# Sliding-window attention and a SwiGLU block: the second half of the output weights issued directly behind the first

## The chip, the cores and the metric

The kernel runs on one core of a Trainium2 chip. The core has five engines that work side by side, each through its own queue, strictly in order: TensorE (PE in the profile; PEld is its weight load), VectorE (DVE), ScalarE (ACT), GpSimd (POOL) and SyncE (SP). Sixteen DMA engines move data between the device's memory and the on-chip memory. The metric is the device time of one execution in microseconds.

## The reference

Two stages follow one another. The first is attention with a sliding window of 128 positions and a linear bias, over 8 batches, 8 heads, 576 positions and a head width of 64:

```
scores = q @ k^T / sqrt(64) - slope[head] * |i - j|, only where 0 <= i - j < 128
x = softmax(scores) @ v, brought to [4608 tokens, 512]
```

The second is a gated feed-forward block on those 4608 tokens, with an inner width of 1536:

```
g = x @ w_gate
out = (g * sigmoid(g) * (x @ w_val)) @ w_out
```

Inputs and output are 32-bit floats; the kernel computes in 16-bit floats and accumulates in 32 bits.

## The kernel before, in words

**Attention.** The sequence is cut into tiles of 128 positions. Two batches together make 9 tiles (four of each batch, and a ninth that holds the last 64 positions of both), so the 8 batches give 36 tiles, numbered 0 to 35 ("rank" in the code). For every tile the kernel loads k, q and v (`load_qk`, L187 to L192, and `load_v`, L182 to L185). k and q have to be transposed. Tiles 0 to 10 are transposed by TensorE (`transposed`, L198 to L223, with the products at L218); from tile 11 on, a DMA transpose does it, issued by SyncE (L239). Then come the scores (L278 and L313), the exponential on ScalarE (L284, L317), the weighting with v (L345), the division on VectorE (L348), and the transpose of the result into xT (L371 or L367).

**Feed-forward.** Tokens go in 9 blocks of 512. Each block has 12 strips of the inner width; a strip is one gate product and one value product (L397), an activation (L415) and two VectorE operations (L416, L427). Block 0's output product is done plainly (`project`, L446 to L457): 12 products per output tile with the 12 strips of w_out, taken from the last strip to the first:

```
m = NMB - 1 - i if n == 0 else i
nc.tensor.matmul(po, hT[n][:, m, j * P:(j + 1) * P], wo_sb[:, m, :],
```

So block 0 reads strips 11 to 6 of `wo_sb` first (its second half by position, `wo_sb[:, 6:12]`), and then strips 5 to 0. Later blocks use a scheme with seven products in place of eight (`strassen`, L504, products at L532); it needs sums of the output weights, which VectorE makes from both halves (`weight_sums`, L468 to L478).

**The order of the work.** The loads of the first eleven tiles and of all weights are issued by GpSimd, in an order that is written out by hand (L876 to L909). Each load names its destination, and the built program lets it wait for what that destination still needs: k and q go into five buffers each in turn, v into twelve. Each load also reports its completion on one of eight semaphores in turn; a load waits until the eighth load before it has landed. On the other engines the order of the first part is the order of the code, and later a scheduler has placed the instructions; TensorE's interleaving of attention and feed-forward comes from the counts in `everything` (L936 to L971). From tile 11 on, `loads_to` (L779) adds a tile's loads as attention proceeds.

The two halves of the output weights are 768 KB each on the chip (128 partitions, 6 strips, 512 columns, 16 bits). The first to be loaded is `wo_sb[:, 6:12]` (L902). Then k and q of tile 9 and q of tile 10 are loaded, then `wo_sb[:, 0:6]` (L905), then v of tile 9, and k and v of tile 10.

Of the kernel before, what the change touches and what calls it, by code (L numbers as in the profile page):

```python
# [51 lines left out]
def kernel(  # L52
# [10 lines left out]
    nc = tc.nc  # L63
# [69 lines left out]
    wo_sb = consts.tile([P, NMB, DM], FP16, name="wo_sb")  # L133
    wg2 = moe_w_gate.rearrange("(kb p) f -> p kb f", p=P)
    wv2 = moe_w_val.rearrange("(kb p) f -> p kb f", p=P)
    wo2 = moe_w_out.rearrange("(a p) d -> p a d", p=P)
# [36 lines left out]
    def source(src, rank):  # L173

        s, c = divmod(rank, 9)
        if c == 8:
            return [((64 * n, 64 * n + 64),
                     src[2 * s + n, :, 512:576, :].rearrange("h p d -> p h d")) for n in range(2)]
        b, t = 2 * s + c // 4, c % 4
        return [((0, P), src[b, :, t * P:(t + 1) * P, :].rearrange("h p d -> p h d"))]  # L180

    def load_v(rank):  # L182
        va[rank] = va_all[rank % NV]
        for (p0, p1), src in source(v, rank):
            nc.gpsimd.dma_start(va[rank][p0:p1, :, 0:D], src)  # L185

    def load_qk(rank, which="kq"):  # L187
        for name in which:
            t_ = nat.tile([P, H, D], FP16, name=name + "n", tag=name + "n")
            for (p0, p1), src in source(k if name == "k" else q, rank):  # L190
                nc.gpsimd.dma_start(t_[p0:p1], src)  # L191
            (natk if name == "k" else natq)[rank] = t_  # L192

    def load(rank):
        load_qk(rank)
        load_v(rank)
# [703 lines left out]
    load_v(7)  # L900
    load(8)
    nc.gpsimd.dma_start(wo_sb[:, 6:12, :], wo2[:, 6:12, :])  # L902
    load_qk(9)
    load_qk(10, "q")
    nc.gpsimd.dma_start(wo_sb[:, 0:6, :], wo2[:, 0:6, :])  # L905
    load_v(9)
    load_qk(10, "k")
    load_v(10)
# [96 lines left out]
```

## Time and profile before

| | us |
|---|---|
| median of 4 runs | 346.74 (346.18 to 348.81) |
| profiled execution, its own time | 345.66 |
| its span, first to last instruction | 343.9 |
| TensorE busy | 330.2 (96%) |
| VectorE busy | 277.3 (81%) |
| ScalarE busy | 207.6 (60%) |
| GpSimd busy (issuing loads) | 109.6 (32%) |
| output weights, issue to landing, median of the two halves | 8.7 |
| k or q of a tile (128 KB), issue to landing, median | 8.5 |

The granted TensorE clock is 1.0 throughout. The DMA engines are busy for 9 tenths or more in each of the first 20 of the span's 40 equal slices, that is for about 172 us, and little afterwards. Busy times overlap between engines and do not add up to the span. In the chain that ended last, a piece of an engine or of a transfer says what released the next instruction, not how long that instruction stood still; how long it stood is in the list of waits. In a row of the timeline the columns are start, length, engine, line, operation, output <- inputs, count, and in brackets the engine's idle time just before the row and what ended it.

### The profile page before, as it was taken

To read this page: it belongs to the slowest core of one execution; us is meant where nothing else is said; L and a number is where in the kernel's file an instruction comes from. 1 tells how busy PE (TensorE), PEld (TensorE's weight loads), DVE (VectorE), ACT (ScalarE), POOL (GpSimd) and SP (SyncE) were. 2 spreads that over 40 slices of the span, in tenths; PEclk is the share of its full clock that TensorE was granted. 3 is DMA by queue.
4 is the path that set the end of the run, shared out by engine and by line. 5 is a ranking of instruction groups with operands and counts; after the bars stand their busy time and mean duration, and the time that the engine had idled before them with its cause. 6 is when DMAs were issued, how large, how long until landed. Compare 5 with 4: busy or idle time off the path is not lost.

```text
span 343.9 us, 7777 instructions
## 1 busy us (share of the span) xinstructions
PE 330.2 (96%) x2983; PEld 219.0 (64%) x2983; DVE 277.3 (81%) x652; ACT 207.6 (60%) x412; POOL 109.6 (32%) x136
## 2 busy tenths in 40 slices
PE   7999989999999999999999999999999999999995
PEld 4484445444456565556565655565788878888884
DVE  5577885999798679998899999999855975775683
ACT  3758676465766665656556547563467666676640
POOL 8977590748855075743017000000000000000000
PEclk9999999999999999999999999999999999999999
DMA  9999999999999999999949914021101101011024
GB/s 151 168 180 175 161 173 149 99 137 180 126 171 150 162 149 171 152 154 149 196 112 92 183 36 79 15 64 45 63 2 61 62 0 64 8 56 63 0 71 115
DMA packets 160037, 37.37 MB, mean 109 GB/s; under 512 B 147328, under 2 KB 155648, under 8 KB 160000
## 3 DMA queue, kind: packets, MB, share of 16 engines
q0 software_dynamic: 118336, 18.62, 85.2%
q1 hardware_dynamic: 40976, 17.64, 27.7%
q10 hardware_dynamic: 688, 0.62, 0.6%
q8 instruction: 23, 0.38, 0.5%
q14 instruction: 14, 0.11, 0.2%
HBM read 37.91 MB, written 9.44 MB: 138 GB/s over the span
## 4 chain that ended last, share of the span: by engine, by line
PE 70%; DVE 18%; ACT 5%; issue 3%; DMA 3%; POOL 0%; DVEq 0%; ACTq 0%
PE po L532 14%; PE pg L397 12%; PE pv L397 12%; PE gX L623 8%; PE gY L623 4%; PE av L345 3%; DVE hT L427 3%; DVE uu L416 3%; DMA wo_sb<-in_moe_w_out_dram 3%; PE ps L278 3%; PE p L532 3%; PE gZ L623 2%; PE po L451 2%; ACT ex L284 2%; DVE x L348 2%
## 5 line engine op out<-in xcount | busy, mean ns | idle before, releaser
L397 PE MATMUL pv<-xT,wv_sb 128*128 128x512 f16 (+2 forms) x320 | 76.5, 358 | 0.6 <-DVE uu L416 0.3
L397 PE MATMUL pg<-xT,wg_sb 128*128 128x512 f16 (+2 forms) x320 | 75.8, 358 | 0.3 <-DVE xT L373 0.2
L415 ACT ACTIVATE tt<-pg 128x512 f16<-128x512 f32 (+2 forms) x70 | 41.3, 590 | 50.5 <-PE pg L397 49.5
L284 ACT ACTIVATE ex<-ps 128x512 f16<-128x512 f32 x96 | 50.0, 606 | 11.8 <-PE ps L278 11.8
L416 DVE SCALAR_TENSOR_TENSOR uu<-tt,pg 128x512 f16<-128x512 f16 (+2 forms) x69 | 46.0, 667 | 10.4 <-ACT tt L415 10.2
L427 DVE TENSOR_TENSOR hT<-uu,pv 128x512 f16<-128x512 f16 (+2 forms) x70 | 46.7, 667 | 3.3 <-PE pv L397 1.6
L185 POOL DMA_DIRECT2D va<-in_v_dram x40 | 34.4, 865 | 38.8 <-PE av L345 30.5
L397 PEld LDWEIGHTS <-wg_sb 128*128 128x128 f16 x320 | 28.2, 98 | 24.4 <-issue 2.2
L397 PEld LDWEIGHTS <-wv_sb 128*128 128x128 f16 x320 | 28.3, 98 | 24.1 <-issue 3.0
L532 PEld LDWEIGHTS <-hT 128*128 128x128 f16 x384 | 36.8, 98 | 10.4 <-issue 1.1
L191 POOL DMA_DIRECT2D kn<-in_k_dram x39 | 33.5, 862 | 22.2 <-DMA kT<-kn 13.8
L191 POOL DMA_DIRECT2D qn<-in_q_dram x39 | 33.6, 866 | 15.1 <-DMA va<-in_v_dram 11.1
L532 PEld LDWEIGHTS <-S 128*128 128x128 f16 x288 | 27.7, 98 | 10.6 <-issue 2.5
L290 DVE TENSOR_TENSOR ex<-ex,m_reg 128x1024 f16<-128x1024 f16 x42 | 28.7, 688 | 3.2 <-ACT ex L284 3.1
L348 DVE TENSOR_TENSOR x<-av,rec 128x256 f16<-128x256 f32 x72 | 28.5, 419 | 0.4
L532 PE MATMUL po<-T,S 128*128 128x256 f16 x192 | 26.5, 273 | 0.5 <-DVE S L487 0.5
L532 PE MATMUL po<-T,hT 128*128 128x256 f16 x192 | 26.1, 273 | 0.0
L317 ACT ACTIVATE exc<-psc 128x512 f16<-128x512 f32 x40 | 21.3, 608 | 4.1 <-PE psc L313 4.1
L675 DVE TENSOR_TENSOR hT<-s,v 128x512 f16<-128x512 f16 x18 | 7.6, 424 | 18.5 <-ACT s L674 18.5
L345 PEld LDWEIGHTS <-ex 128*128 128x128 f16 x384 | 17.4, 97 | 4.6 <-issue 1.3
L345 PE MATMUL av<-va,ex 128*128 128x65 f16 x384 | 19.3, 194 | 0.7 <-ACT ex L284 0.7
L278 PE MATMUL ps<-qT,kT 64*128 64x256 f16 x192 | 16.6, 273 | 0.4 <-DVE qT L223 0.2
(134 smaller groups left out, 537.7 us busy)
## 6 DMA issues: line engine op xcount, KB each, us to landing
out_dram<-osb SPq DMA_DIRECT2D x32, 256.0 KB, 2.7
va<-in_v_dram POOLq DMA_DIRECT2D x32, 128.0 KB, 8.9
qn<-in_q_dram POOLq DMA_DIRECT2D x31, 128.0 KB, 8.5
kn<-in_k_dram POOLq DMA_DIRECT2D x31, 128.0 KB, 8.5
wg_sb<-in_moe_w_gate_dram POOLq DMA_DIRECT2D x6, 256.0 KB, 7.7
wv_sb<-in_moe_w_val_dram POOLq DMA_DIRECT2D x6, 256.0 KB, 8.2
wo_sb<-in_moe_w_out_dram POOLq DMA_DIRECT2D x2, 768.0 KB, 8.7
kn<-in_k_dram POOLq DMA_DIRECT2D x8, 64.0 KB, 7.4
```

What stands on the lines that cost most here:

```text
L185: nc.gpsimd.dma_start(va[rank][p0:p1, :, 0:D], src)
L191: nc.gpsimd.dma_start(t_[p0:p1], src)
L284: nc.scalar.activation(e[:, o:o + 2, :], banks[q4][par], AF.Exp, scale=scale)
L290: nc.vector.tensor_mul(e[:, o, :], e[:, o, :], reg[:, o, :])
L345: nc.tensor.matmul(av[:, j, :], w, val, start=(n == 0), stop=(n == len(todo) - 1))
L348: nc.vector.tensor_mul(x[:, 4 * half:4 * half + 4, :], av[:, :, 0:D], rec.broadcast_to([P, 4, D]))
L397: nc.tensor.matmul(ps[:, c0:c1], w[:, kb, ms], xT[n][:, kb, c0:c1], start=(kb == 0 and c0 == 0), stop=(kb == NKB - 1 and c1 == 512), skip_ ...
L415: nc.scalar.activation(tt, pg[:, c0:c1], AF.Tanh, scale=0.5)
L416: nc.vector.scalar_tensor_tensor(out=uu, in0=tt, scalar=one if (n, m) == PIN else 1.0, in1=pg[:, c0:c1], op0=ALU.add, op1=ALU.mult)
L427: nc.vector.tensor_mul(hT[n][:, m, c0:c1], acted[(n, m)][1][:, c0:c1], pv[:, c0:c1])
L532: nc.tensor.matmul(dst, a[:, m, cols], b[:, m, :], start=(start and m == 0), stop=(m == HM - 1), skip_group_check=True)
L623: nc.tensor.matmul(dst[:, i, :], w[:, kb, c0 + i * P:c0 + (i + 1) * P], a[:, kb, :], start=(start and i == 0 and kb == 0), stop=(i == 1 an ...
```

## The change

One line of the hand-written order moves up by two lines: the load of `wo_sb[:, 0:6]` is issued directly behind that of `wo_sb[:, 6:12]`, ahead of k and q of tile 9 and q of tile 10. Nothing else of the code changes. On GpSimd four loads change places; the order of instructions on the other engines stays as it was, and where one of them waits for one of these four loads, it waits on the semaphore of the load's new place.

```
     load_v(7)
     load(8)
     nc.gpsimd.dma_start(wo_sb[:, 6:12, :], wo2[:, 6:12, :])
+    nc.gpsimd.dma_start(wo_sb[:, 0:6, :], wo2[:, 0:6, :])
     load_qk(9)
     load_qk(10, "q")
-    nc.gpsimd.dma_start(wo_sb[:, 0:6, :], wo2[:, 0:6, :])
     load_v(9)
     load_qk(10, "k")
     load_v(10)
```

More of the change, by code (lines that the diff above doesn't have):

```diff
@@ L902 @@
     nc.gpsimd.dma_start(wo_sb[:, 6:12, :], wo2[:, 6:12, :])
+    nc.gpsimd.dma_start(wo_sb[:, 0:6, :], wo2[:, 0:6, :])
     load_qk(9)
     load_qk(10, "q")
-    nc.gpsimd.dma_start(wo_sb[:, 0:6, :], wo2[:, 0:6, :])
     load_v(9)
```

## The prediction

> **What bounds the kernel now.** I read the page first: how full each engine is, and what the chain that ended last consists of.
>
> ```profile
> PE 330.2 (96%) x2983; PEld 219.0 (64%) x2983; DVE 277.3 (81%) x652; ACT 207.6 (60%) x412; POOL 109.6 (32%) x136
> PE 70%; DVE 18%; ACT 5%; issue 3%; DMA 3%; POOL 0%; DVEq 0%; ACTq 0%
> ```
>
> TensorE is busy 96% of the 343.9 us, and 70% of the chain is its own work. A transfer is worth time only where TensorE stands waiting for it. The chain does contain one long transfer, and it is the one that this change moves; so the second view is the chain in order of time, around it.
>
> ```profile
> 43.48 1.40 POOL qn L191 x2
> 44.88 0.33 issue
> 45.21 9.51 DMA wo_sb<-in_moe_w_out_dram
> 54.72 0.04 issue
> 54.76 0.59 PE po L451 x2
> ```
>
> The piece of 9.51 us looks like the prize (2.8% of the span). It isn't one: the chain is followed back from whatever released an instruction last, however short the wait. The waits of TensorE between 40 and 60 us give the real size:
>
> ```profile
> PE px L371 <- DVE x L348: 0.8, 2, 0.6
> PE psc L313 <- ACT xT L375: 0.2, 1, 0.2
> PE po L451 <- DMA wo_sb<-in_moe_w_out_dram: 0.2, 1, 0.2
> ```
>
> One wait of 0.2 us. For nearly all of the 9.51 us TensorE had other work. Fourth view: the GpSimd queue, which issues every load and which the change reorders.
>
> ```profile
> 40.56 0.84 POOL L902 DMA_DIRECT2D wo_sb<-in_moe_w_out_dram  x1 [0.72 <-DMA wv_sb<-in_moe_w_val_dram]
> 42.60 0.88 POOL L191 DMA_DIRECT2D kn<-in_k_dram  x1 [1.21 <-PE ps L278]
> 43.48 1.76 POOL L191 DMA_DIRECT2D qn<-in_q_dram  x2
> 45.21 0.85 POOL L905 DMA_DIRECT2D wo_sb<-in_moe_w_out_dram  x1
> 46.02 0.92 POOL L185 DMA_DIRECT2D va<-in_v_dram  x1
> ...
> 48.90 0.88 POOL L191 DMA_DIRECT2D kn<-in_k_dram  x1 [0.21 <-PE av L345]
> 49.76 0.88 POOL L191 DMA_DIRECT2D qn<-in_q_dram  x1
> ```
>
> The first kn and the two qn are k of tile 9 and q of tiles 9 and 10; the last two rows are k and q of tile 11. Fifth view: when TensorE takes the things that trade places.
>
> ```profile
> 54.01 0.59 PE L451 MATMUL po<-wo_sb,hT 128*128 128x512 f16 x2
> 54.76 0.59 PE L451 MATMUL po<-wo_sb,hT 128*128 128x512 f16 x2 [0.15 <-DMA wo_sb<-in_moe_w_out_dram]
> 55.30 0.39 PE L218 MATMUL pt<-idm,kn 128*128 128x128 f16 x4
> 55.52 0.39 PE L218 MATMUL pt<-idm,qn 128*128 128x128 f16 x4
> 56.29 0.39 PE L218 MATMUL pt<-idm,qn 128*128 128x128 f16 x4
> ```
>
> The row at 54.76 is the first to use the half that is moved. Half a microsecond later come the transposes of k 9 and q 9, then q 10. So the change helps one use and endangers three right behind it on the same in-order engine.
>
> **The landings.** Issue plus time to landing, one load at a time: first half of the weights 40.56 + 7.8 = 48.4; k 9 42.60 + 6.6 = 49.2; q 9 43.48 + 6.6 = 50.1; q 10 44.34 + 6.5 = 50.9; second half 45.21 + 9.5 = 54.7; v 9 46.02 + 9.8 = 55.8; k 10 57.5; v 10 58.5; k 11 48.90 + 10.3 = 59.2; q 11 59.7; v 11 60.7. They land in the order of issue and the DMA engines read 9 tenths throughout: one backlog, worked off in order. What one load occupies is the distance between landings: the second half 54.7 - 50.9 = 3.8 us, and k 9, q 9, q 10 0.8, 0.9 and 0.8, together 2.5.
>
> **Part 1: the second half of the weights earlier (gain 0.25 us).** In the new order it waits for the completion of the eighth load before it (the built program puts each load on one of eight semaphores in turn). That is v 7, 33.01 + 9.1 = 42.1. It is issued at about 42.1 and joins a backlog that has 6 us left, so it follows the first half directly: 48.4 + 3.8 = 52.2 instead of 54.7. TensorE wants it at 54.4 (the pair at 54.01 at a pitch of 0.59 - 0.38 = 0.21 us each), so the wait goes. Its size is 0.15 us counted from the modelled end of the matmul before, 0.32 from the pitch. Next in line are the transposes of x at L371, whose input the trace has ready at 54.7, which caps the gain at 0.28. I take 0.25; below nothing is excluded for this term, since the wait only ends earlier.
>
> **Part 2: k 9, q 9, q 10 later (cost 0).** Behind the weights they land at 52.2 + 0.8 = 53.1, 53.9 and 54.7. TensorE, 0.25 us earlier than now, wants them at 55.0, 55.25 and 56.0. Margins: 1.9, 1.3 and 1.3 us. The cover is what TensorE does up to then; if it is gone, each microsecond of lateness is one of span, as TensorE is in order.
>
> [...]
>
> **Part 3: GpSimd's queue (cost 0).** One issue of 0.85 us moves ahead of three. GpSimd idles 1.21 us at that point anyway, waiting for TensorE to free k 9's buffer; the weights' issue fills 42.1 to 43.0, and k 9, q 9, q 10 are issued 0.4 us later, v 9 0.4 us earlier. All stand in the backlog for over 6 us, so this moves no landing.
> The turn of semaphores adds one wait: the load of q 11 waits for its eighth predecessor, which was k 9 (landed 49.2) and becomes the second half of the weights (52.2). So q 11 is issued at 52.3, not 49.76, and v 11 at about 53.2; behind them is k 12, which waits for the transpose of k 11 until 62.38 anyway. Their data's turn comes only after k 11, at 59.2. The shortest landing of such a load in this stretch is 3.5 us (the one issued at 62.38): 52.3 + 3.5 = 55.8, still ahead of its turn. Cost 0 by that row; from the other end, if it kept today's 9.9 us it would land at 62.2, and SyncE's transpose of q 11, now at 60.71, would slip 1.5 us. I take 0: the 9.9 is time in a backlog, not of the load.
> The queue of SyncE keeps its order; its first transpose (59.30) waits for k 11, which has the same bytes ahead of it as before. VectorE first reads the moved half at 60.40 (L475): no gain there. The order on TensorE and ScalarE is unchanged.
>
> **Sum.** -0.25 + 0 + 0: the profiled execution (span 343.9, with 1.76 around it 345.66) becomes 345.4. The median of the four runs is 346.74, 1.08 above that execution; the same difference gives 346.5.
>
> **Rivals.**
> - The gain is swallowed: from 57 us on there are waits on ScalarE and VectorE that do not move (ACT tt <- PE pg and the like), and a lead of 0.25 us can end in one of them. Then 346.7. Against it: the stretch from 57.1 to 70 us is gap-free on TensorE.
> - Slower: k 9, q 9 or q 10 come late to L218. It decides once q 10 lands after 56.0 or q 9 after 55.25, that is once the weights and the three loads together take 1.3 us more than 3.8 + 2.5. [...] For it: a pair of 768 KB loads back to back isn't in the trace. Against it: a row of each load and a steady pace.
> - GpSimd held up at q 11 pushes the transposes of tile 11 by up to 1.5 us: 348.2. Against it: the backlog of over 6 us behind which it hides.
> - The chain's 9.51 us is really won, at least in part: more than 3.5 us. Against it: the single wait of 0.2 us.
>
> **Chances.** As forecast 0.65; swallowed 0.20; late k and q 0.10, of which 0.06 beyond 1%; GpSimd held up 0.03; chain's gain 0.02. A measurement of this kernel can tell about 1% from no change (its runs go from 346.18 to 348.81), so nearly all of this is "same": faster 0.02, same 0.92, slower 0.06. The range takes the forecast and the swallowed gain with the scatter of the runs, about 1 us below, and above it the bound at q 11 and mild lateness: 345.4 to 348.3.
>
> **What would show it.** Right: the wait po <- wo_sb of 0.2 us is gone from TensorE; the second half lands near 52.2; k 9, q 9, q 10 land near 53.1, 53.9, 54.7; GpSimd shows an idle stretch before q 11 of about 3 us ended by wo_sb; k 11 still lands near 59.2. Wrong: a wait of TensorE at L218 on kn or qn, a first transpose on SyncE clearly after 59.3, or a different course of the loads after 62 us.

## The result, and the profile after

The changed kernel takes 345.10 us, the median of 44 executions (344.75 to 345.64). The kernel before, run beside it, takes 346.18 us, the median of 63 (345.23 to 349.11). The ratio of the means is 0.9952, 95% interval 0.9940 to 0.9963: 0.5% faster. The forecast was 346.5 us and the range began at 345.4, so the change won more than was foreseen. As striking as the median is the spread: the executions of the kernel before cover 3.9 us, those of the changed one 0.9 us.

The page of the changed kernel, its engines and its chain:

```profile
PE 329.4 (96%) x2983; PEld 218.4 (64%) x2983; DVE 277.5 (81%) x652; ACT 207.7 (61%) x412; POOL 109.6 (32%) x136
PE 70%; DVE 19%; ACT 6%; issue 3%; DMA 1%; ACTq 0%; DVEq 0%
```

The share of transfers in the chain falls from 3% to 1%: the piece of 9.51 us isn't in it any more. The span falls from 343.9 to 343.1 us. The waits of TensorE between 40 and 60 us in the changed kernel:

```profile
PE px L371 <- DVE x L348: 0.8, 2, 0.6
PE psc L313 <- ACT xT L375: 0.2, 1, 0.2
```

The wait for `wo_sb` is gone and no new one has come. The GpSimd queue of the changed kernel:

```profile
40.58 0.84 POOL L902 DMA_DIRECT2D wo_sb<-in_moe_w_out_dram  x1 [0.67 <-DMA wv_sb<-in_moe_w_val_dram]
42.30 0.83 POOL L903 DMA_DIRECT2D wo_sb<-in_moe_w_out_dram  x1 [0.88 <-DMA va<-in_v_dram]
43.11 0.89 POOL L191 DMA_DIRECT2D kn<-in_k_dram  x1
43.98 1.77 POOL L191 DMA_DIRECT2D qn<-in_q_dram  x2
...
52.80 0.88 POOL L191 DMA_DIRECT2D qn<-in_q_dram  x1 [2.84 <-DMA wo_sb<-in_moe_w_out_dram]
```

The second half is issued at 42.30 and lands 10.2 us later, at 52.5. The stall before q of tile 11 is there (2.84 us, ended by the weights' landing) and costs nothing. And TensorE in the changed kernel, at the place in question:

```profile
53.65 1.02 PE L451 MATMUL po<-wo_sb,hT 128*128 128x512 f16 x4
54.51 0.28 PE L371 MATMUL px<-idm,x 128*128 128x128 f16 x2
54.62 0.39 PE L218 MATMUL pt<-idm,kn 128*128 128x128 f16 x4
54.85 0.39 PE L218 MATMUL pt<-idm,qn 128*128 128x128 f16 x4
...
55.62 0.39 PE L218 MATMUL pt<-idm,qn 128*128 128x128 f16 x4
```

The four products run without a gap. The transposes follow at 54.62, 54.85 and 55.62, on data that landed at 53.47, 54.42 and 55.36: in time, but by 0.3 us in the last case.

Laid side by side, product by product, the two profiles differ by two steps only. TensorE is 0.37 us earlier from 7.7 us on, and at the waiting product of L451 the lead jumps to 0.68 us (54.76 against 54.08). It then stays at 0.67 to 0.68 us to the end.

The change has no part in the first step, nor do the loads: the first two land at 3.96 and 5.70 us before, at 4.08 and 5.78 us after. It is TensorE's clock. The profile's record of the clock begins, at full speed, at 7.02 us in the kernel before and at 4.85 us in the changed one, so the "1.0 throughout" said above holds from there on. In between run the following two products (before, then after):

```profile
5.00 1.06 PE L208 MATMUL pt<-kT 128*128 128x512 f16 x2
4.98 0.59 PE L208 MATMUL pt<-kT 128*128 128x512 f16 x2
```

The two stretches less the 0.63 and 0.38 us of one product make 0.43 us from start to start against 0.21: half speed against full.

Since the second step is kept to the end, what TensorE gains at this place goes undiminished into the time.

### The profile page after: what moved, and what is told of

Its sections match the earlier page's. It is cut to its first block, busy times and chain, and to the rows that moved or that the text cites. A ratio compares the mean times of both kernels' runs of the same rounds, so it can differ in the third digit from the quotient of the medians.

```text
span 343.1 us, 7778 instructions
## 1 busy us (share of the span) xinstructions
PE 329.4 (96%) x2983; PEld 218.4 (64%) x2983; DVE 277.5 (81%) x652; ACT 207.7 (61%) x412; POOL 109.6 (32%) x136
## 4 chain that ended last, share of the span: by engine, by line
PE 70%; DVE 19%; ACT 6%; issue 3%; DMA 1%; ACTq 0%; DVEq 0%
PE po L532 15%; PE pg L397 13%; PE pv L397 12%; PE gX L623 8%; PE gY L623 4%; PE av L345 4%; DVE uu L416 3%; DVE hT L427 3%; PE ps L278 3%; PE p L532 2%; PE po L451 2%; PE gZ L623 2%; DVE x L348 2%; ACT ex L284 2%; PE px L371 2%
## 5 line engine op out<-in xcount | busy, mean ns | idle before, releaser
L416 DVE SCALAR_TENSOR_TENSOR uu<-tt,pg 128x512 f16<-128x512 f16 (+2 forms) x69 | 46.0, 667 | 10.4 <-ACT tt L415 10.2
```

Source lines behind the costliest of these rows:

```text
L416: nc.vector.scalar_tensor_tensor(out=uu, in0=tt, scalar=one if (n, m) == PIN else 1.0, in1=pg[:, c0:c1], op0=ALU.add, op1=ALU.mult)
```

## The experiments

The second half is called "the weights" in what follows. The question was where the rest of the gain comes from: the first profile showed a wait of 0.15 us, the medians moved by 1.1 us and the means by 1.67.

### The kernel before, again

No edit.

> The kernel before once more, unchanged, for a second profile of it and its spread of times. Theory W (the gain is TensorE's wait for the second half of the output weights, and that wait is longer in many executions than the 0.15 us of the first profile): executions near 347 and 349 us turn up again, and a profile of a longer execution shows the wait at L451 longer by just so much. Rival B (the wait is 0.3 us in every execution, the rest of the gain arises later, in the loads after 60 us): the wait stays near 0.15 us and a longer execution loses its time after 60 us.

Measured: 346.06 us median (22 executions, 345.51 to 348.89). Its profile is of an execution of 347.35 us, 1.69 us longer than the first profile's. TensorE's longest wait in it, between 38 and 66 us:

```profile
PE po L451 <- DMA wo_sb<-in_moe_w_out_dram: 2.2, 1, 2.2
```

Product by product, this execution is 0.36 us ahead of the first profile up to the waiting product, 1.63 us behind it there, and so to the end. The whole difference between the two executions is this wait. Theory W stands; rival B, which had the wait constant, falls.

The 53 executions of the kernel before that ran beside this one fall into three groups. 24 take 345.4 to 346.4 us (mean 345.86). 14 take 346.8 to 347.7 (mean 347.20), like the one profiled here. 15 take 348.2 to 349.2 (mean 348.72), and exactly these 15 have a mean granted clock of 0.994 or 0.995, where all others have 0.997 or more.

### The weights one place later

```
     load_qk(10, "q")
+    load_v(9)
     nc.gpsimd.dma_start(wo_sb[:, 0:6, :], wo2[:, 0:6, :])
-    load_v(9)
```

> The second half one place later than before, behind v of tile 9. W: it lands 1.1 us later (55.8 by the first profile), the wait at L451 grows from 0.15 to about 1.2 us, the median grows by about 1.1 us (ratio 1.003). B: less than 0.5 us, since the order of the loads behind is nearly the same.

Measured: 348.76 us median (8 executions, 347.43 to 349.18), ratio to the kernel before 1.0065 (1.004 to 1.009). That is more than W expected, and the profile, of an execution of 348.97 us, says why. The wait is 2.2 us. Behind it, by stages (columns: stage, its length, busy time and instructions of TensorE, of its weight load, of VectorE, ScalarE and GpSimd, then the granted TensorE clock, DMA, GB/s):

```profile
54.00:56.00 2.00, 0.66 (x10) 0.26 (x7) 1.68 (x6) 0.42 (x1) 0.00 (x0) 1.00 1.96 172
56.00:58.00 2.00, 1.19 (x11) 0.95 (x11) 0.00 (x0) 0.00 (x0) 0.00 (x0) 0.84 2.43 154
58.00:60.00 2.00, 2.00 (x13) 1.28 (x12) 0.50 (x2) 1.08 (x2) 0.00 (x0) 0.50 1.22 77
60.00:62.00 2.00, 2.00 (x9) 0.84 (x8) 0.35 (x1) 0.96 (x3) 0.00 (x0) 0.81 0.36 70
```

The clock falls to half from 57.35 to 60.76 us, half a microsecond after TensorE has resumed. In that time TensorE falls from 2.05 to 3.53 us behind the first profile: 1.5 us more, without any wait. So a wait for the weights has two prices: its length, and at times another 1.5 us for the clock. Seven of these 8 executions show the low clock (0.994 or 0.995); the eighth took 347.43 us at 0.999. By clock and time the third group of the kernel before is the same thing, though no execution of that group was profiled.

In these traces a stretch at full clock lasts a whole number of times 3.413 us: 337.92 us in the profiles of the kernel before and of the changed one (99 times), 51.20 and 286.72 us here (15 and 84 times), with one slow stretch of 3.41 us in between. Cut into pieces of that length, counted from the start of the full clock, the profile with the weights one place later (first two rows) and the one of the kernel before, again (last row), look like this:

```profile
53.94:57.35 3.41, 1.25 (x15) 0.61 (x13) 1.74 (x6) 0.48 (x1) 0.00 (x0) 1.00 2.13 166
57.35:60.76 3.41, 3.41 (x22) 2.24 (x20) 0.85 (x2) 1.17 (x2) 0.00 (x0) 0.50 1.21 81
52.47:55.88 3.41, 1.77 (x24) 1.03 (x25) 2.51 (x7) 1.54 (x4) 0.00 (x0) 1.00 1.77 181
```

In the first, TensorE is idle for 2.16 us of one piece, and the next piece has half the clock. In the second, the wait is as long, but two pieces meet at 55.88 us, within it: 1.64 us of idle time fall in front, and the clock stays at 1.00. In the first profile of the kernel before it stays too, behind a piece with 1.90 us of idle time (338.11 to 341.52 us). So a wait of about 2 us halved the clock in one execution and not in another. That it depends on where the wait falls against these pieces is my estimate from these idle times; no run tested it. Their position differs between executions: the full clock is on record from 7.02 us in the kernel before and from 4.85 in the changed one.

### The weights one place earlier

```
     load_qk(9)
+    nc.gpsimd.dma_start(wo_sb[:, 0:6, :], wo2[:, 0:6, :])
     load_qk(10, "q")
-    nc.gpsimd.dma_start(wo_sb[:, 0:6, :], wo2[:, 0:6, :])
```

> The second half one place earlier than before, ahead of q of tile 10 alone. W: it lands 0.8 us earlier (53.9), just before TensorE wants it at 54.1 to 54.4, so the wait in a fast execution goes (0.3 us less) and long executions become fewer or shorter by 0.8 us: median between the two kernels, 345.3 to 345.8. B: 0.3 us less at most and the long executions stay.

Measured: 345.16 us median (22 executions: 21 from 344.68 to 345.87, one of 348.97 at a clock of 0.995), ratio 0.9958 (0.9939 to 0.9978). One place recovers nearly all of the gain, a little more than W expected. Its profile is of one of its longer executions, 345.70 us, in which the wait has moved to q of tile 10:

```profile
PE pt L218 <- DMA qn<-in_q_dram: 0.7, 1, 0.7
```

### k and q later still

The changed order, with v of tile 9 put ahead of k and q:

```
     nc.gpsimd.dma_start(wo_sb[:, 0:6, :], wo2[:, 0:6, :])
+    load_v(9)
     load_qk(9)
     load_qk(10, "q")
-    load_v(9)
```

> As the changed kernel, but v of tile 9 is also put ahead of k and q of tiles 9 and 10, which land about 1 us later than in the changed kernel (54.5, 55.4 and 56.4 against 53.5, 54.4 and 55.4 there). TensorE wants them at 54.6, 54.8 and 55.6 there. If k and q have the small margin that the profile of the changed kernel shows (1.1, 0.4 and 0.2 us), a wait at L218 of about 0.8 us appears and the median rises by 0.5 to 1.0 us over the changed kernel's. If there is more margin in most executions, less than 0.3 us.

Measured: 346.55 us median (14 executions, 345.52 to 347.12), 1.4 us above the changed kernel and level with the kernel before that ran beside it (ratio 0.9999, 0.9979 to 1.0019). The waits of TensorE in its profile, of its longest execution:

```profile
PE pt L218 <- DMA qn<-in_q_dram: 1.4, 2, 0.9
...
PE pt L218 <- DMA kn<-in_k_dram: 0.4, 1, 0.4
```

So the prediction's rival of late k and q is real, and the changed kernel escapes it narrowly: one 128 KB load more ahead of them costs 1.4 us. The expectation had 0.5 to 1.0; it counted only the load's own time. In the profile the first two waits, 0.9 us together, are of that size. The third, of 0.9 us, is for q of tile 10, whose landing is reported in 16 parts: 15 had come by 56.99 us, when TensorE was still busy, and the last came at 58.00. The next section is about such late reports. No execution has a low clock (0.998 or more), although 1.8 us of waits have come: TensorE is idle for 0.75 us from 54 to 56 us and for 1.06 from 56 to 58.

### What delays the weights

In all profiles one read of 16 KB falls between 54 and 58 us and takes about 1 us (1.00 in the kernel before, 1.12 in the changed one). It goes through a queue that the page lists as instructions (23 reads, 0.38 MB in all):

```profile
q8 instruction: 23, 0.38, 0.5%
```

Each load is complete when 16 reports have come (3872 for 242 transfers in the profile of each of the two kernels). The times of the last three, drawn from the traces (us):

```
kernel                 read at   load that it meets   last three reports
before, first profile  55.34     k 10                 56.4  56.5  57.5
before, again          54.23     the weights          55.4  55.5  56.3
weights one later      54.45     the weights          55.6  55.6  56.8
weights one earlier    54.43     q 10                 55.1  55.1  56.6
changed kernel         54.97     v 9                  56.4  56.4  57.3
```

Each time one single report lags by 0.8 to 1.5 us, and so it does in the loads queued just behind. The traces don't name the DMA engine of a report or of the read; that it is one in 16 suggests one engine of the 16, the one that would be busy with the read. A lag can have other causes too: in the profile of the run in two pieces, below, one report is 0.6 us late from 49.3 us on, ahead of the read at 54.96. In the first profile of the kernel before, the weights (reports up to 54.5, 54.6, 54.7) were complete before the read began; in the second they were not. In the changed kernel everything that TensorE wants before 56 us is ahead of the bytes that it holds up. In the profiles of the two kernels the read recurs every 89 to 156 products of TensorE (23 reads in 2983 products), so it is likely that it brings TensorE's own instructions.

Theory F says that the wait is long where this read comes ahead of the weights' last bytes; its rival P says that only the pace of the transfers varies and the read plays no part. To tell them apart, the fillers that TensorE runs at the start to pass the time were altered, since they shift its stream of instructions. Fewer fillers, in the order of loads of the kernel before:

```
-IDLE = {("k", 0): 0, ("q", 0): 2}
-REPEAT = {("q", 1): 4, ("k", 1): 2}
+IDLE = {("k", 0): 0, ("q", 0): 4}
+REPEAT = {}
```

> The order of loads of the kernel before. Of TensorE's fillers at the start 14 are left out (28 instructions: 16 repeated transposes out, two wide products in), so that the read of instructions comes about 1 us later in the program, after 55.3 us. F: the second half lands ahead of the read in most executions, the executions above 346.7 become fewer than half of what they are in the kernel before, median about 346. P: no change of the spread. Fewer fillers may leave TensorE's clock lower at the start, which would show as a different granted clock or a constant offset before 10 us.

Measured: 346.01 us median (14 executions, 345.68 to 346.27), none of them above 346.7, while beside it the kernel before had a median of 347.02 (345.25 to 349.09) and 30 of 58 executions above 346.7. The read comes at 56.45, after the weights have landed (55.35). The wait in its profile is still there:

```profile
PE po L451 <- DMA wo_sb<-in_moe_w_out_dram: 1.0, 1, 1.0
```

TensorE's own start doesn't explain this: it is ready for the waiting product at 54.22 us, between the 54.07 and 54.44 of the two profiles of the kernel before. So the pace of the transfers alone makes a wait of up to 1 us: the first group. That the read adds what leads to the other two groups is what F expected, and P, with an unchanged spread, did not. The same fillers with the weights one place later (C is the theory that part of the loss is the halved clock):

> The second half behind v of tile 9 (348.76 us median with the usual fillers, 7 of 8 executions at a granted clock of 0.994 or 0.995) together with the fillers of the run in which the read of TensorE's instructions came later (14 products fewer at the start). Theory F with C: the read again comes behind the second half, which lands at about 55.7 to 56.3 instead of 56.8; the wait at L451 is 1.2 to 2.0 us, and executions with the low clock become the exception; median 346.8 to 347.6. Rival P (the read plays no part): as with the usual fillers, within 0.3 us of 348.76, most executions at the low clock.

Measured: 346.76 us median (22 executions, 346.05 to 350.41), against 348.76 with the usual fillers; 13 of the 22 have a clock of 0.999 or more, and take 346.05 to 346.93. In its profile the read (55.69) no longer holds up the weights (last reports 55.8, 55.8, 56.1), though the wait is still 2.0 us and the clock drops; that execution took 348.41. Rival P expected 348.76 within 0.3 us and most executions at the low clock, which are 9 of 22 here; F had expected them to be the exception, which is true only in part. The 2.0 us between the two medians overstate the effect, because the runs come from different batches: above the kernel before in its own batch, the mean is 0.8 us with these fillers and 1.65 us with the usual ones (ratios 1.0025, 1.0003 to 1.0046, and 1.0065, 1.004 to 1.009). The two runs also differ in TensorE's start. So the read is supported as a cause by the run with fewer fillers and by the late reports, but its share is not measured.

Three more runs don't decide the question. The first has the order of loads of the kernel before, with more fillers (four of the seven wide ones at the start replaced by 18 narrow ones, and `REPEAT` raised to 6 and 3):

> The order of loads of the kernel before. Among TensorE's fillers at the start, 26 small products more (52 instructions), which bring nothing new: the 16 KB read of TensorE's next instructions, which the profiles show at 54.2 to 55.4 us on one of the DMA engines (1 us long), should come about 2 us earlier in the program. Theory F (that read holds up one DMA engine's share of everything queued behind it, and the wait is long in the executions where it comes ahead of the second half's last bytes): the second half always lands late, about 55.5 or more, the wait at L451 is 1 us or more in nearly every execution, short executions (under 346.5) become rare, median 347 or more. Rival P (the wait varies with the pace of the DMA engines alone, the read plays no part): the spread and the median stay those of the kernel before, within 0.3 us.

Measured: 347.80 us median. In the profile the repeated transposes take 2.72 us for 24 in place of 1.05 for 16, twice as long for each: the record of the full clock begins only at 12.98 us, in place of 7.02. TensorE starts its scores 3.2 us late, the weights have long landed when it comes to them, and the read is at the same place in the program as before. So it says nothing on F. It does show the other side of the balance: TensorE 3.2 us late has no wait, and the time grows by 2.7 us in place of 3.2.

The same fillers with the changed order of loads:

> The changed order of loads with the 52 more filler instructions. F: now the read of instructions falls ahead of the last bytes of k 9, q 9 and q 10 and holds them up by up to 1 us; a wait at L218 of 0.3 to 0.9 us, median 0.3 to 0.8 us above the changed kernel's, and no execution with a wait at L451. P: as the changed kernel within 0.2 us.

Measured: 345.99 us median (22 executions, 345.48 to 349.10); in its profile TensorE starts 0.65 us late, there is no wait at L218 or L451, and the read (54.97) again meets only v of tile 9. It says nothing on F either. Nine of its executions take 347.5 us or more at a clock of 1.000; they may be late starts like that of the run before, but none of them was profiled.

The order of loads of the kernel before, with only the fillers at the very start altered:

```
-        for _ in range(n):
+        for _ in range(n - 3):
             nc.tensor.matmul(t_, idle[:, 0:P], idle, start=True, stop=True)
+        for _ in range(14):
+            nc.tensor.matmul(t_[:, 0:64], idle[:, 0:P], idle[:, 0:64], start=True, stop=True)
```

> The order of loads of the kernel before; of the seven fillers at the very start three are replaced by 14 narrow ones of about the same length, so that TensorE's stream has 22 instructions more in front and its start is not disturbed. Theory F: if the read of instructions moves, it comes about 1 us earlier in the program, the second half is caught more often, and executions above 346.7 become three quarters or more of all. P: about half of them, as in the kernel before (29 of 53). If the profile shows the read at the same place in the program, the run says nothing on F.

Measured: 346.88 us median (14 executions, 346.21 to 349.58), 9 of them above 346.7, but the short ones are longer too. The profile, of the longest, has the read at 54.00 and a wait of 2.4 us with the clock at half for 3.4 us, the same picture as with the weights one place later. The read hasn't moved in the program (it comes behind 502 products, the 11 added ones left out, against 505 and 510 in the two profiles of the kernel before), so by its own condition the run doesn't decide. What sets the moment of the read stays open.

### Filling the wait

The order with the weights one place later, and in `project`, ahead of the waiting product:

```
                 m = NMB - 1 - i if n == 0 else i
+                for _ in range(8 if (n, j, i) == (0, 0, 6) else 0):
+                    nc.tensor.matmul(po, idle[:, 0:P], wo_sb[:, NMB - 1, :], start=False, stop=False)
```

> The order of loads of the run in which the second half came behind v of tile 9 (348.76 us median there, 7 of 8 executions at a granted clock of 0.994 or 0.995), with 8 products more on TensorE just ahead of the product that waits: each multiplies by zeros and adds nothing, 0.215 us each, 1.7 us in all, inside a wait that was 2.2 us. Theory C (part of the loss is TensorE's clock, halved after a wait of about 2 us): the wait in the profile shrinks to about 0.5 us, no execution shows a clock below 0.997, median 347.0 to 347.5, that is 1.3 to 1.7 us faster although TensorE has more to do. Rival D (the executions near 349 wait longer for data and their clock figure only follows from that): median and clocks as without the products, 348.5 or more.

Measured: 352.31 us median (6 executions). The scheduler placed the products elsewhere: the profile shows them spread over 54 to 67 us between other work, and the waiting products moved to 67 us. It is another kernel, and decides nothing on the wait at L451. Theory C rests on the profile with the weights one place later, where TensorE has no wait from 57.35 to 60.76 us and loses 1.5 us at a clock of 0.50, and on the groups above.

### The weights in two pieces

The changed order, with the last-used third of the weights behind q of tile 10:

```
-    nc.gpsimd.dma_start(wo_sb[:, 0:6, :], wo2[:, 0:6, :])
+    nc.gpsimd.dma_start(wo_sb[:, 2:6, :], wo2[:, 2:6, :])
     load_qk(9)
     load_qk(10, "q")
+    nc.gpsimd.dma_start(wo_sb[:, 0:2, :], wo2[:, 0:2, :])
```

> The second half in two pieces: strips 2 to 5 directly behind the first half, strips 0 and 1 behind q of tile 10. By the landings of the changed kernel's profile: strips 2 to 5 at 51.1, k 9, q 9, q 10 at 52.1, 53.0 and 54.0 (1.3 us earlier than there), strips 0 and 1 at 55.3, wanted at 55.8. Theory W: no wait of TensorE on any of them, median that of the changed kernel or up to 0.2 us less (345.0), with no execution above 346. If the last piece is caught by the read of instructions, a wait of up to 0.5 us at its place.

Measured: 344.97 us median (22 executions, 344.68 to 345.41), ratio to the kernel before 0.9948 (0.9933 to 0.9964). There is no wait on any of the pieces. k 9, q 9 and q 10 land at 52.8, 53.6 and 54.4, the last piece at 55.7. It is the lowest median of the kernels tried, but 0.13 us from the changed kernel, which ran in another batch, is less than these runs can tell. What it buys is margin for q 10, which lands 0.9 us earlier: 1.5 us in place of 0.3 in the two profiles, of which 0.3 us are a later TensorE.

## Why the prediction was wrong

**The size of part 1 failed, and with it the last step of the sum.** The mechanism was right: the wait on the second half goes, nothing takes its place, the gain reaches the end whole. But the 0.25 us was the wait of one execution, and a short one. (Even there 0.32 us were won, as the pitch had said; the cap of 0.28 from the input of L371 didn't hold.) Two things were hidden in that profile.

First, TensorE came to full clock late in it, and its start was 0.37 us later than in most other profiles. At a place where TensorE waits for a transfer, a late start shortens the wait and costs nothing. The time was set by the landing of the weights, not by TensorE's own pace. Taking the wait away frees the lead as well: 0.32 + 0.36 = 0.68 us between the two profiles, not far from the 0.80 us between the short executions of the kernel before and the changed kernel. The chain with its 9.51 us had said this in its way: TensorE and the transfers were nearly level. I read it as saying nothing.

Second, "the median of the four runs is 346.74, 1.08 above that execution; the same difference gives 346.5". That difference wasn't a constant around the program. It was the same wait, longer. The 63 executions that ran beside the changed kernel fall into the same three groups: 38 up to 346.50 us (mean 345.90), 12 from 346.86 to 347.83 (347.29), 13 from 348.60 (348.83). From their mean to that of the changed kernel, 346.77 - 345.10 = 1.67 us divide thus: 0.80 from the first group's level, which all share; 12 of 63 times another 1.39, which is 0.26; 13 of 63 times another 2.93, which is 0.60. Half of the gain is from executions that the profile didn't show. The four times given, 346.18, 346.18, 347.31 and 348.81, had two of the first group and one of each other.

**Part 2 was right in its outcome, with luck in its margins.** The landings came 0.4 to 0.7 us later than forecast and TensorE wanted them 0.4 us earlier, so margins of 1.9, 1.3 and 1.3 us were 1.1, 0.4 and 0.3. The rival of late k and q decided where it was said to: one load more ahead of them costs 1.4 us. Behind the weights too, k 9, q 9 and q 10 land 0.94 to 0.96 us apart. No run shows the loss beyond 1% at this place that was given a chance of 0.06: the 1.4 us are 0.4%.

**Part 3 was right.** The stall before q 11 is 2.84 us, where about 3 was forecast; q 11 lands at 60.3. k 11 lands at 59.8 in place of 59.2 and SyncE's first transpose starts at 59.90 in place of 59.30. I had named a later transpose as a sign of error; it has no effect on TensorE, whose lead stays.

**The rival of a swallowed gain fell**, since the lead is kept to the end. The rival of the chain's full 9.51 us fell too: the whole of it came to under 2 us.

## What to carry to other kernels

Where the chain passes through a transfer, ask by how much it would have to be late to matter, not only how long the wait is in this execution: a wait near zero on an engine that is otherwise full means that engine and transfer are level, and a transfer that comes later in another execution adds to the time, as 0.15 us here became 2.15. When the times of a kernel spread more than its engines' work can, take a second profile of a longer execution before sizing a wait. And where a large load competes with others, it can be cut along the order of use: the piece needed first goes first, the rest behind what is needed in between. Here that won margin, not time.

## What the runs showed that was not expected

- A 16 KB read through the instruction queue, about 1 us long, goes with a delay of 0.8 to 1.5 us in one of the 16 reports of the loads queued at that moment, and a load is as late as its last report. What share of the gain this has stays open.
- In three of four profiles with a wait of 2.0 to 2.4 us for the weights (one place later with either set of fillers, and with the fillers at the very start altered) the clock of TensorE was halved behind it for about 3.4 us; with the usual fillers and the weights one place later this cost another 1.5 us. In the fourth, of the kernel before, again, the clock stayed at 1.00, as it did with waits of 1.8 us in all for k and q.
- The mean granted clock of an execution shows this from outside: of all 157 executions of the kernel before that ran beside the experiments, the 42 with a clock of 0.995 or less took 348.23 us or more, the other 115 took 348.17 us or less.
